# A two-layer kernel gets a written instruction order for TensorE and SyncE in the rest of its first layer, later stores, a weight reload on another queue, and wider spacing in its attention part

## The chip, the cores and the metric

One NeuronCore of one Trainium2 chip runs the whole program. The metric is device microseconds of that core, from launch to end; a lower number is better. Engines run side by side, each taking its own instructions in the order in which the program holds them: TensorE (PE in the profile, its weight loads PEld), VectorE (DVE), ScalarE (ACT), GpSimd (POOL) and SyncE (SP), which here only issues transfers. A DMA queue belongs to the engine that issues it.

## The reference, cut to what matters

```python
kv  = einsum('bhsd,bhse->bhde', k, v)            # 8 batches, 8 heads, 576 tokens, 64 wide
out = einsum('bhsd,bhde->bhse', q, kv)
x   = out / sqrt(mean(out*out, -1) + 1e-6) * g_norm    # then (4608 tokens, 512)
h   = x @ w_in;   x = (h * sigmoid(1.702 * h)) @ w_out       # layer 0: 512 -> 2048 -> 512
h   = x @ w2_in;  y = (h - tanh(h)) @ w2_out                 # layer 1: the same sizes
```

## The kernel before, in words

The 4608 tokens are eight superblocks of 576 (`T`; `H` is half of it), one per batch. The program runs layer 0 over superblocks 0 to 7, then layer 1 over the same eight: `for l in range(2): for n in range(NS)` (L876). Between the layers the activations wait in HBM (`x2d`).

**The two matrix stages.** Each matrix product is done on 2 x 2 blocks with seven block products in place of eight, and each operand is split into a float16 high and low part, so a block product is three matmuls of 128 x 288 (high by high, high by low, low by high). `m1` (L520) is the first matrix of a superblock: 54 steps of six matmuls, each into one of the PSUM tiles X, Y, Z, and two more steps (`tail1`, `tail2`) that are emitted among the first steps of the next stage. Its weights `wi[0..7]` stay in SBUF. After a step ACT copies X out (L563), DVE adds Y or Z to a copy (L568), and ACT applies the layer's function into `GT` (L537, L541). `m2` (L635) is the second matrix: 28 steps of twelve matmuls (L702 to L704). Its right operands `jt` are made from `GT` by DVE (`jA`, L591), ACT (`jB`, L605) and DVE again (`jC`, L611), emitted up to six steps ahead in a ring of seven. Its weights are streamed from HBM: `stream` (L629) loads half of a block into one of four slots `st`, 14 loads a superblock, each waiting until TensorE has read the slot's last content. A load emitted in step i is first used about seven steps later. `fin` closes a block product: ACT scales it into a buffer of `mscr`, DVE adds (L650), `store` sends it to `x2d` on SP's queue in layer 0 and to the output `outT` on GpSimd's in layer 1 (L647).

**Side work.** Generators hold the rest of the work; each `yield` is a turn. `tick(0)` after every step of `m1` and `tick(1)` after every step of `m2` give each generator its rate of turns (`add_side(g, rate in m1, rate in m2)`), and what a turn emits stands behind the latest main instruction of the same engine (`issue_after`). In layer 0, `front(b)` is the attention of batch b: four units, each five matmuls for k by v (L385, recorded as ten), two turns, two matmuls by q (L397, recorded as four), ACT squares and copies (L409 to L411), a turn, a DVE subtraction (L413), two turns, four matmuls that sum squares (L421). `back(b)` (L473) is its normalisation: the inverse root (`newton`, L441), then per unit two matmuls that spread it over the partitions (`scaled_unit`, L456) into `AT`, two DVE multiplications that read `AT` (L460), and after every second unit the seven sums and the split that make the next superblock's operand `xo` (`xprep`, L306). From superblock 2 on, `back(n + 1)` runs in `m1` at rate 0.6 and `front(n + 2)` in `m2` at rate 1.1. In superblock 0 both run for batch 1, at 0.15 turns a tick in its first stage and 2.5 in its second, in superblock 1 for batch 2. `conv1` converts layer 1's weights in the `m1` stages from superblock 2 on, with loads and stores on GpSimd's queue, and leaves them in HBM (`wid`, `wod[1]`). After the last `m2` of layer 0, eight transfers of 896 KB on SP's queue bring `wid` into `wi` (L947 to L949).

**What sets the order.** The program is built with a planner that simulates a timeline and picks each engine's order from it, within dependencies. Where `tc.manual_schedule(engines=...)` is open, the named engines keep the order in which the program emits their instructions. Before, that holds for PE and SP in layer 1 alone (L908 to L912):

```python
            if l == 1:
                fixed[0] = True
                ...
                man.enter_context(tc.manual_schedule(engines=frozenset([mybir.EngineType.PE, mybir.EngineType.SP])))
```

Of the kernel before, what the change touches and what calls it, by code (L numbers as in the profile page):

```python
# [21 lines left out]
NS = NTOK // T  # L22
H = T // 2
NP = 8
# [58 lines left out]
def body(ctx, tc, att, gn, con, w_in, w_out, w2_in, w2_out, outT):  # L83
# [217 lines left out]
    def main(ins):  # L301

        latest[ins.ins.engine] = ins.ins
# [51 lines left out]
    def fetch(b):  # L355

        kb = yield from part(b, 0, T, UNIT)
        qb = yield from part(b, 0, 0, T)
        ahead[b] = qb, kb
# [113 lines left out]
    def back(b, dst):  # L473

        hi, hl = shr[:, 0:H], slr[:, 0:H]
        yield from newton(slice(0, P), hi, hl)
        for x in yt:
            x.free()
        for u, (kt, i) in enumerate(UNITS):
            yield from scaled_unit(b, u, hl, slice(0, P), AT)  # L480
            if i == 1:
                ex = yield from scr.need(3 * H)
                yield from xprep(xbs[b, kt], ex, dst[:, kt])
                if kt == 0 and b < NS - 1:
                    yield from fetch(b + 1)


    side, fixed = [], [False]
# [146 lines left out]
    def m2(l, n, tails, pre):  # L635
        inv = 1.0 / (SX * SW[1])
        cc = {}
        tail1, tail2, flush = tails
        LA = NJ - 2

        def store(qd, ob, ds):

            m, j = qd // 2, qd % 2
            src = ob.ap[:, :T].rearrange("p (d f) -> p d f", d=2)[:, ds]
            dst = (x2d if l == 0 else outT.rearrange("(k p) f -> k p f", p=P))
            dst = dst[2 * m:2 * m + 2, :, n * T + j * H:n * T + (j + 1) * H].rearrange("d p f -> p d f")[:, ds]
            main((nc.sync if l == 0 or n == NS - 1 else nc.gpsimd).dma_start(out=dst, in_=src))  # L647

        def fma(out, ps, b):
            main(nc.vector.scalar_tensor_tensor(out=out, in0=ps, scalar=inv, in1=b, op0=ALU.mult, op1=ALU.add))  # L650

        def scaled(ps, d, name):
            if d == 0:
                cc[name] = mscr(T)
            o = cc[name].ap[:, d * H:(d + 1) * H]
            main(nc.scalar.activation(out=o, in_=ps, func=AF.Copy, scale=inv))
            return o

        def quad(qd, d, name):
            if (l, n) == (1, NS - 1):  # L660
                store(qd, cc[name], slice(d, d + 1))
            elif d == 1:
                store(qd, cc[name], slice(0, 2))
            if d == 1:
                cc.pop(name).free()

        def fin(r, d):
            x, y, z = X[d][:, 0:H], Y[d][:, 0:H], Z[d][:, 0:H]
            if r == 1:
                o = scaled(x, d, 1)  # L670
                fma(o, y, o)
                quad(0, d, 1)
            elif r == 6:
                o = scaled(x, d, 6)
                fma(o, z, o)
            elif r == 7:
                o = scaled(x, d, 7)
                fma(o, z, o)
                quad(3, d, 7)
            elif r == 3:  # L680
                o = cc[6].ap[:, d * H:(d + 1) * H]
                fma(o, y, o)
                quad(1, d, 6)
            elif r == 4:
                scaled(x, d, 4)
                quad(2, d, 4)

        for i in range(28):
            r, pp = STEPS2[i]
            s = pre[ORDER2.index(r) * 2 + pp // 2]  # L690
            jadvance(i + 1)
            j = jbuf.pop(i)
            bank = {2: Y, 1: X, 5: Z, 6: X, 7: X, 3: Y, 4: X}[r]
            fresh = r in (2, 1, 5, 3)
            k = not fresh
            for d in range(2):
                out = bank[d][:, 0:H]
                for p in range(2):
                    wh, wl = (s[:, pp % 2 * 2 + p, d, t, :] for t in range(2))
                    xh, xl = (j[:, p, t, :] for t in range(2))  # L700
                    a, z = fresh and i == FIRST2[r] and p == 0, i == LAST2[r] and p == 1
                    nc.tensor.matmul(out=out, lhsT=wh, rhs=xh, start=a, stop=False, skip_group_check=k)  # L702
                    nc.tensor.matmul(out=out, lhsT=wh, rhs=xl, start=False, stop=False, skip_group_check=k)  # L703
                    nc.tensor.matmul(out=out, lhsT=wl, rhs=xh, start=False, stop=z, skip_group_check=k)  # L704
                if i == LAST2[r]:
                    fin(r, d)
            for _ in range(min(FREED2.get(i, 0), 14 - len(pre))):
                pre.append(stream(l, len(pre)))
            if i == 0:
                tail1()  # L710
            elif i == 1:
                tail2()
            elif i == 2:
                flush()
                flush()
                jcap[0] = 28
            jadvance(i + 1 + LA)
            tick(1)


    QW = {(0, 0): 1, (0, 1): 2, (1, 0): 3, (1, 1): 0}
# [154 lines left out]
    for l in range(2):  # L876
        for n in range(NS):
            bk = fr = None
            if l == 0:
                if n == 0:  # L880
                    bk = add_side(both(1, xo[1]), 0.15, 2.5)
                elif n == 1:
                    bk = add_side(both(2, xo[0]), 1.5, 0.8)
                elif n < NS - 1:
                    bk = add_side(back(n + 1, xo[(n + 1) % 2]), 0.6, 1.0)
                else:
                    bk = add_side(x2load(0, xo[0]), 0.4, 0.8)
            elif n < NS - 1:
                bk = add_side(x2load(n + 1, xo[(n + 1) % 2]), 0.4, 0.8)
            if (l, n) == (0, 2):  # L890
                add_side(later, 0.85, 0.0)

            def hook(p):
                if (l, n) == (0, 0):
                    adv((16, 18, 20, 21, 22, 23, 24, 25)[p])
                    if p == 2:
                        withdraw(extra)
                    return
                if (l, n) == (0, 1):
                    upto(p + 2)  # L900
                if p >= 2 and p % 2 == 0:
                    jcap[0] = (1, 2, 5)[p // 2 - 1]
                    jadvance(jcap[0])

            jpos[:] = [0, 0, 0]
            jcap[0] = 0
            man = ExitStack()
            if l == 1:  # L908
                fixed[0] = True
                marks.clear()  # L910
                marks.update({k: m for k, m in latest.items() if k == mybir.EngineType.DVE})
                man.enter_context(tc.manual_schedule(engines=frozenset([mybir.EngineType.PE, mybir.EngineType.SP])))  # L912
            if (l, n) == (0, 0):
                m1_plain(hook)
                adv(32)
                k4 = lambda t, n: [t[:, k * 1024:k * 1024 + 1024] for k in range(n)]
                dfr = []
                late = k4(jx, 2)

                def start_sums():  # L920
                    for p in range(NP):
                        for h in range(2):
                            nc.sync.dma_start(out=wod[0][0:3, :, p, h].rearrange("r q t f -> q r t f"), in_=wi[p][:, h, 4:7])
                    for p in range(0, NP, 4):
                        nc.sync.dma_start(out=wod[0][3, :, p:p + 4], in_=w3[:, p:p + 4])
                    spare.extend(k4(cbk, 3) + k4(stf, 2) + late)
                    dfr.append(add_side(sums(), 1.5, 0.7))
                m2_plain()
                drain([bk])
                barred.extend(late)  # L930
                spare[:] = [x for x in spare if all(x is not e for e in late)] + k4(stf[:, 2048:4096], 2)
                closed.append(1)
                jn[0] = sn[0] = 0
                continue
            if (l, n) == (0, 1):
                upto(2)
            tails = m1(l, n, hook)
            if (l, n) == (0, 1):
                drain(dfr)
            jcap[0] = 5  # L940
            pre = [stream(l, i) for i in range(4)]
            if l == 0 and 1 <= n < NS - 2:
                drain([bk])
                fr = add_side(front(n + 2), 0.0, 1.1)
            m2(l, n, tails, pre)
            if l == 0 and n == NS - 1:
                drain([later])  # L947
                for p in range(NP):
                    nc.sync.dma_start(out=wi[p], in_=wid[p])  # L949
            drain([bk, fr])  # L950
            man.close()

# [40 lines left out]
```

## Time and profile before

| | |
|---|---|
| median of 3 runs | 1512.32 us (1511.89 to 1515.27) |
| the profiled execution's own time | 1515.95 us |
| its span, first to last instruction | 1514.2 us |
| TensorE busy | 1459.4 us (96%), 11508 matmul records |
| VectorE, ScalarE, GpSimd busy | 1184.3 us (78%), 945.7 us (62%), 134.7 us (9%) |
| mean granted TensorE clock | 0.981 of full speed |

The profile is of one execution. Times in it count from the first instruction. A matmul's recorded length (0.29 us) is longer than the distance to the next one's start, since matmuls overlap; the pace is read from start to start. In rows with an idle time, it stands in brackets with what ended it. Layer 0 ends and layer 1 begins near 851 us; superblock 2 of layer 0 begins near 285 us.

### The profile page before, as it was taken

How to read it: one execution, taken by the hardware profiler on the slowest of the kernel's cores; microseconds unless marked ns; L12 is line 12 of the kernel's file. 1: busy time of each engine (PE TensorE's matmuls, PEld its weight loads, DVE VectorE, ACT ScalarE, POOL GpSimd, SP SyncE). 2: the span in 40 equal slices, each digit the busy share in tenths (PEclk: the TensorE clock that was granted, in tenths of full speed). 3: DMA queues.
4: the chain of work that ended last, by engine and by line, in shares of the span. 5: the costliest groups of instructions: out<-in, count | busy, mean ns of one | idle time of the engine just before them, and what ended most of it. 6: DMA issues, size and time to landing. Idle time of an engine off the chain costs nothing.

```text
span 1514.2 us, 29446 instructions
## 1 busy us (share of the span) xinstructions
PE 1459.4 (96%) x11508; PEld 1159.8 (77%) x11508; DVE 1184.3 (78%) x2357; ACT 945.7 (62%) x2075; POOL 134.7 (9%) x209
## 2 busy tenths in 40 slices
PE   6979799999999999999999999999999999999999
PEld 5667577777787877877677777777777777777777
DVE  4999979497796987959858686877777787868585
ACT  5766586676777767767556465646565565656463
POOL 0000010022223221211100000000000000000000
PEclk8899899999999999999999999999999999999999
DMA  8684415447567475672576415070614333241504
GB/s 310 208 249 128 147 62 196 140 132 250 165 209 234 128 253 178 199 237 70 185 250 231 148 59 192 15 231 22 195 56 156 111 118 125 86 142 44 184 15 157
DMA packets 96525, 235.36 MB, mean 155 GB/s; under 512 B 10112, under 2 KB 49152, under 8 KB 96384
## 3 DMA queue, kind: packets, MB, share of 16 engines
q1 hardware_dynamic: 78848, 165.95, 34.1%
q0 software_dynamic: 17536, 67.51, 13.4%
q8 instruction: 90, 1.47, 0.4%
q14 instruction: 51, 0.42, 0.1%
HBM read 191.48 MB, written 41.94 MB: 154 GB/s over the span
## 4 chain that ended last, share of the span: by engine, by line
PE 78%; DMA 8%; DVE 8%; ACT 3%; issue 3%; POOL 0%; SPq 0%; ACTq 0%; DVEq 0%; POOLq 0%
PE X L530 7%; PE X L702 7%; PE X L704 7%; PE X L703 7%; PE X L532 7%; PE X L531 7%; PE Y L702 4%; PE Y L704 4%; PE Y L703 4%; PE Z L530 3%; PE Z L532 3%; PE Z L531 3%; DMA st<-wod 3%; PE Z L702 2%; PE Z L704 2%
## 5 line engine op out<-in xcount | busy, mean ns | idle before, releaser
L611 DVE SCALAR_TENSOR_TENSOR jt<-gt,jt 128x576 f16<-128x576 f32 x420 | 312.6, 753 | 106.9 <-ACT jt L605 103.1
L605 ACT ACTIVATE jt<-gt 128x576 f16<-128x576 f32 x420 | 284.6, 684 | 156.0 <-PE X L704 56.6
L530 PE MATMUL X<-xo,wi 128*128 128x288 f16 x960 | 274.6, 286 | 7.4 <-ACT mscratch L563 4.7
L531 PE MATMUL X<-xo,wi 128*128 128x288 f16 x960 | 274.7, 286 | 2.1 <-DVE xo L323 2.1
L532 PE MATMUL X<-xo,wi 128*128 128x288 f16 x960 | 274.6, 286 | 0.0
L703 PE MATMUL X<-jt,st 128*128 128x288 f16 x960 | 274.2, 286 | 0.0
L704 PE MATMUL X<-jt,st 128*128 128x288 f16 x960 | 274.0, 286 | 0.0
L702 PE MATMUL X<-jt,st 128*128 128x288 f16 x960 | 273.4, 286 | 0.0
L702 PEld LDWEIGHTS <-st 128*128 128x128 f16 x1680 | 165.0, 98 | 60.8 <-DMA st<-wod 17.2
L563 ACT COPY mscratch<-X 128x288 f32<-128x288 f32 x360 | 141.2, 396 | 106.1 <-PE X L532 92.6
L531 PEld LDWEIGHTS <-wi 128*128 128x128 f16 x1680 | 164.7, 98 | 50.4 <-issue 8.2
L530 PEld LDWEIGHTS <-wi 128*128 128x128 f16 x1680 | 164.5, 98 | 47.1 <-issue 4.4
L703 PEld LDWEIGHTS <-st 128*128 128x128 f16 x1680 | 165.1, 98 | 43.4
L704 PEld LDWEIGHTS <-st 128*128 128x128 f16 x1680 | 165.2, 98 | 43.4 <-issue 0.3
L532 PEld LDWEIGHTS <-wi 128*128 128x128 f16 x1680 | 164.5, 98 | 44.3 <-issue 2.5
L591 DVE TENSOR_TENSOR gt<-gt 128x576 f32<-128x576 f32 x240 | 176.7, 749 | 1.4 <-ACT gt L537 1.1
L702 PE MATMUL Y<-jt,st 128*128 128x288 f16 x480 | 136.2, 289 | 10.3 <-DMA st<-wod 10.3
L568 DVE TENSOR_TENSOR mscratch<-Z,mscratch 128x288 f32<-128x288 f32 x240 | 108.1, 452 | 38.5 <-ACT mscratch L563 22.2
L703 PE MATMUL Y<-jt,st 128*128 128x288 f16 x480 | 137.9, 288 | 0.0
L704 PE MATMUL Y<-jt,st 128*128 128x288 f16 x480 | 137.5, 288 | 0.0
L530 PE MATMUL Z<-xo,wi 128*128 128x288 f16 x480 | 137.5, 286 | 0.0
L531 PE MATMUL Z<-xo,wi 128*128 128x288 f16 x480 | 137.4, 286 | 0.0
(238 smaller groups left out, 2572.0 us busy)
## 6 DMA issues: line engine op xcount, KB each, us to landing
st<-wod SPq DMA_DIRECT2D x210, 512.0 KB, 4.7
scratch<-att POOLq DMA_DIRECT2D x28, 640.0 KB, 4.8
scratch<-x2d SPq DMA_DIRECT2D x32, 288.0 KB, 5.9
cbk<-w_out POOLq DMA_DIRECT2D x32, 256.0 KB, 4.3
cbk<-w_in POOLq DMA_DIRECT2D x32, 256.0 KB, 4.1
scratch<-att POOLq DMA_DIRECT2D x28, 288.0 KB, 4.5
x2d<-mscratch SPq DMA_DIRECT2D x28, 288.0 KB, 5.4
outT<-mscratch POOLq DMA_DIRECT2D x28, 288.0 KB, 5.0
```

The source lines that it names most:

```text
L530: nc.tensor.matmul(out=out, lhsT=wh, rhs=xh, start=fresh and kt == 0, stop=False, skip_group_check=k)
L531: nc.tensor.matmul(out=out, lhsT=wh, rhs=xl, start=False, stop=False, skip_group_check=k)
L532: nc.tensor.matmul(out=out, lhsT=wl, rhs=xh, start=False, stop=kt == 1, skip_group_check=k)
L563: main(nc.scalar.copy(out=b.ap, in_=x))
L568: main(nc.vector.tensor_tensor(out=b.ap, in0=add[0], in1=b.ap, op=ALU.add))
L591: tt = lambda o, a, b: main(nc.vector.tensor_tensor(out=G[:, :, o, :], in0=G[:, :, a, :], in1=G[:, :, b, :], op=ALU.subtract))
L605: main(nc.scalar.activation(out=j[:, :, 0, :], in_=GT[STEPS2[i][1]][:, :, QD[STEPS2[i][0]], :], func=AF.Copy, scale=SX))
L611: main(nc.vector.scalar_tensor_tensor(out=j[:, :, 1, :], in0=GT[STEPS2[i][1]][:, :, QD[STEPS2[i][0]], :], scalar=SX, in1=j[:, :, 0, :], op ...
L702: nc.tensor.matmul(out=out, lhsT=wh, rhs=xh, start=a, stop=False, skip_group_check=k)
L703: nc.tensor.matmul(out=out, lhsT=wh, rhs=xl, start=False, stop=False, skip_group_check=k)
L704: nc.tensor.matmul(out=out, lhsT=wl, rhs=xh, start=False, stop=z, skip_group_check=k)
```

## The change

- From superblock 2 of layer 0 on (`n >= 2`), PE and SP keep the order of emission, as in layer 1.
- In layer 0 a `store` is no longer emitted where its block product is finished: it is put on a list and emitted three steps later, behind that step's weight loads (`due`); the last one at the stage's end. Its buffer is given back then.
- `back` gets two more turns after `newton` and one more after each unit (six in all); its rate in `m1` from superblock 2 to 6 is 0.72 in place of 0.6.
- The reload of `wi` between the layers is a generator on GpSimd's queue, given 0.4 turns a step during the last `m2` of layer 0, in place of eight transfers on SP's queue emitted after it; what is left of `conv1` is emitted before that `m2`, not after it.

```diff
@@ back
         for x in yt:
             x.free()
+        yield
+        yield
         for u, (kt, i) in enumerate(UNITS):
             yield from scaled_unit(b, u, hl, slice(0, P), AT)
+            yield
             if i == 1:
...
+    def reload():
+
+        for p in range(NP):
+            nc.gpsimd.dma_start(out=wi[p], in_=wid[p])
+            yield
@@ m2, store
-            main((nc.sync if l == 0 or n == NS - 1 else nc.gpsimd).dma_start(out=dst, in_=src))
+            if l == 0:
+                late.append((step_[0] + 3, dst, src, ob))
+            else:
+                main((nc.sync if n == NS - 1 else nc.gpsimd).dma_start(out=dst, in_=src))
@@ m2, quad
-                cc.pop(name).free()
+                ob = cc.pop(name)
+                if l == 1:
+                    ob.free()
@@ m2
+        step_, late = [0], []
+
+        def due(i):
+            while late and late[0][0] <= i:
+                _, dst, src, ob = late.pop(0)
+                main(nc.sync.dma_start(out=dst, in_=src))
+                ob.free()
+
         for i in range(28):
+            step_[0] = i
...
             for _ in range(min(FREED2.get(i, 0), 14 - len(pre))):
                 pre.append(stream(l, len(pre)))
+            due(i)
...
             tick(1)
+        due(99)
@@ the loop over superblocks
-                    bk = add_side(back(n + 1, xo[(n + 1) % 2]), 0.6, 1.0)
+                    bk = add_side(back(n + 1, xo[(n + 1) % 2]), 0.72, 1.0)
...
                 man.enter_context(tc.manual_schedule(engines=frozenset([mybir.EngineType.PE, mybir.EngineType.SP])))
+            elif n >= 2:
+                man.enter_context(tc.manual_schedule(engines=frozenset([mybir.EngineType.PE, mybir.EngineType.SP])))
...
-            m2(l, n, tails, pre)
             if l == 0 and n == NS - 1:
                 drain([later])
-                for p in range(NP):
-                    nc.sync.dma_start(out=wi[p], in_=wid[p])
+                fr = add_side(reload(), 0.0, 0.4)
+            m2(l, n, tails, pre)
             drain([bk, fr])
             man.close()
```

## Rows read from the trace of the kernel before

**Rows 1.** The page's head: span, TensorE's busy time, its granted clock in 40 slices.
```profile
span 1514.2 us, 29446 instructions
...
PE 1459.4 (96%) x11508; PEld 1159.8 (77%) x11508; DVE 1184.3 (78%) x2357; ACT 945.7 (62%) x2075; POOL 134.7 (9%) x209
...
PEclk8899899999999999999999999999999999999999
```
**Rows 2.** Stretches: length, each engine's busy us (count), PE's clock, DMA share, GB/s.
```profile
528.00:578.00 50.00, 47.54 (x361) 38.04 (x359) 38.47 (x70) 35.01 (x73) 10.10 (x16) 0.97 0.78 254
1099.00:1472.00 373.00, 373.00 (x3043) 297.49 (x3041) 282.83 (x552) 210.60 (x457) 12.13 (x17) 1.00 0.32 103
```
**Rows 3.** Waits of TensorE from 285 to 851: us in total, times, longest.
```profile
PE Y L702 <- DMA st<-wod: 9.1, 5, 2.5
PE Z L702 <- DMA st<-wod: 4.4, 2, 2.3
PE X L530 <- ACT mscratch L563: 0.4, 2, 0.2
```
**Rows 4.** TensorE's timeline around one of those waits: start, length, instruction.
```profile
736.67 0.32 PE L702 MATMUL Z<-jt,st 128*128 128x288 f16 x1 [2.29 <-DMA st<-wod]
736.80 0.43 PE L703 MATMUL Z<-jt,st 128*128 128x288 f16 x1
...
740.14 0.33 PE L702 MATMUL Z<-jt,st 128*128 128x288 f16 x1
```
**Rows 5.** TensorE's timeline, two more of those waits.
```profile
349.78 0.30 PE L702 MATMUL Z<-jt,st 128*128 128x288 f16 x1 [2.09 <-DMA st<-wod]
...
832.87 0.30 PE L702 MATMUL Y<-jt,st 128*128 128x288 f16 x1 [2.03 <-DMA st<-wod]
833.00 0.29 PE L703 MATMUL Y<-jt,st 128*128 128x288 f16 x1
```
**Rows 6.** The chain of waits, 723 to 742: start, length, what.
```profile
730.61 6.01 DMA st<-wod
```
**Rows 7.** Weight loads (L632), 285 to 851: from issue to landing.
```profile
DMA to landing us min/median/max: 3.7/4.9/8.8
```
**Rows 8.** Waits of SP's queue from 285 to 851: us in total, times, longest.
```profile
SPq L647 <- DVE mscratch L650: 16.1, 13, 3.1
```
**Rows 9.** Timelines of one attention unit: q matmuls on TensorE, subtraction on DVE.
```profile
444.12 1.13 PE L397 MATMUL AT<-scratch,kv 128*128 128x288 f32 x4
448.80 0.75 DVE L413 TENSOR_TENSOR sq<-scratch,sq 128x576 fp32r<-128x576 f32 x1
```
**Rows 10.** The quickest and the slowest such pair, on TensorE and DVE.
```profile
566.51 1.13 PE L397 MATMUL AT<-scratch,kv 128*128 128x288 f32 x4
569.08 0.76 DVE L413 TENSOR_TENSOR sq<-scratch,sq 128x576 fp32r<-128x576 f32 x1 [0.40 <-ACT sq L410]
...
373.40 1.13 PE L397 MATMUL AT<-scratch,kv 128*128 128x288 f32 x4
378.97 0.76 DVE L413 TENSOR_TENSOR sq<-scratch,sq 128x576 fp32r<-128x576 f32 x1 [3.16 <-ACT sq L410]
```
**Rows 11.** Timelines of spread matmuls and the multiplications that read them.
```profile
687.84 0.52 PE L456 MATMUL AT<-sq,sel 128*128 128x288 f32 x2
688.59 0.81 DVE L460 TENSOR_TENSOR scratch<-AT,scratch 128x288 f32<-128x288 f32 x2
...
596.54 0.52 PE L456 MATMUL AT<-sq,sel 128*128 128x288 f32 x2
600.96 0.81 DVE L460 TENSOR_TENSOR scratch<-AT,scratch 128x288 f32<-128x288 f32 x2
```
**Rows 12.** Waits of TensorE from 156 to 236.
```profile
PE X L530 <- ACT mscratch L563: 4.0, 5, 1.8
PE X L531 <- DVE xo L323: 2.1, 1, 2.1
PE X L530 <- ACT xo L320: 2.0, 1, 2.0
```

## The prediction, written before the result was known

> **What bounds the kernel now.** The page first: TensorE is busy 96% of the 1514.2 us span, and its clock is below full in the first fifth alone [rows 1]. Slices hide short losses, so next the table of stretches. In layer 1 TensorE is busy for all of 373.00 us with 3043 matmuls, 0.1226 us each, at full clock [rows 2]. That is the floor for this list of matmuls; layer 1, already in written order, has nothing to give. In layer 0 a stretch of 50 us has 47.54 us of work and a clock of 0.97 [rows 2]: here time is lost.
>
> The waits of TensorE from 285 to 851 us say to what: seven waits for a weight load, 9.1 + 4.4 = 13.5 us, and next to nothing else (0.4 us for ACT) [rows 3]. The chain of waits shows where one comes from: the load was issued at 730.61, the moment its slot was free, and took 6.01 us [rows 6], but TensorE wanted it 2.29 us before 736.67 [rows 4], less than four microseconds after the issue. A step of `m2` is 12 x 0.1226 = 1.47 us, and by emission a load is first used some seven steps after its slot is free, 10.3 us. So the planner's order of matmuls, which starts block products early and interleaves them, uses up the distance that the program had put there.
>
> Each wait has a second price. After 736.67 the matmuls from 736.80 to 740.14 start 0.24 us apart [rows 4], the 1.2 GHz level; then 2.4 GHz comes back. The same follows the waits near 350 (2.09 us), 556 and 654. It does not follow the one of 2.03 us at 832.87 [rows 5]. One such stretch costs half its length, 3.34 / 2 = 1.67 us; four make 6.7 us.
>
> **Part by part.** *PE and SP in order, gain.* The seven waits go if each load has its 10.3 us: landing takes 4.9 us in the median and 8.8 at most [rows 7], so even the slowest has 1.5 us left. I take all of it: 13.5 us of waiting, 6.7 us of clock, 0.4 us for ACT: 20.6 us. What is late next is below.
>
> *Late stores.* On an SP queue in order, a store waiting for DVE would hold the loads behind it. Waits for DVE before a store are at most 3.1 us [rows 8]; three steps are 4.4 us, and the loads of the same step go first. So a store finds its data ready: no cost to the loads. It isn't later for the buffer's next user either, since the last two stores follow the last load and go when their data is there. Zero; were a store still to wait 3.1 us, the load behind would have 8.8 + 3.1 = 11.9 us to fit into 10.3 in the very worst case, 1.6 us each.
>
> *Reload on GpSimd.* Eight issues off SP's queue onto one with 134.7 us of work in 1514.2 [rows 1], given out over 20 of 28 steps; the first has over 30 us before layer 1 reads it, and the slowest landing of a 512 KB load is 8.8 us [rows 7]. Zero, hidden behind the last `m2` of layer 0. Without that cover, layer 1's first step would wait for one landing, up to some 9 us.
>
> *PE in order, price in `front`.* Now the attention's matmuls stand at fixed places. Between q matmuls and square sums lie three turns; at 1.1 turns a step that is three steps in two of the four units and two steps in the other two. With the q matmuls themselves (1.13 us) TensorE comes to the square sums 5.5 or 4.1 us after it began on q. The subtraction they need is done after 569.84 - 566.51 = 3.3 us at best, 379.73 - 373.40 = 6.3 us at worst [rows 10], 5.4 us in an ordinary unit [rows 9]. So a two-step unit waits between nothing and 2.2 us, a three-step unit between nothing and 0.8. There are 16 units from superblock 2 on, eight of each kind. With 0.5 us for the first kind and 0.15 for the second (latencies lie between the ordinary and the best, as ACT and DVE no longer have steps of `m2` begun early to serve): 5 us; bounds 0 and 8 x 2.2 + 8 x 0.8 = 24 us.
>
> The Trainium skill, page "TensorE: Matmul & The Clock Gate", section "Step-by-step: what each phase is for", says that only weight loads are pulled ahead and that matmuls stay in program order. By that rule every matmul behind an unready square sum waits with it, though it could run; this speaks against the change, and is the third rival below. The trace agrees as far as it goes: at 736.67 all of TensorE stood 2.29 us for one operand.
>
> *PE in order, price in `back`.* Each second spread must wait until `AT` is read. At 0.72 turns a step of 6 x 0.1226 = 0.74 us, three turns are about four steps: with the spread's own 0.52 us TensorE is back after 3.5 us. The multiplications end 1.6 us after the spread began where DVE comes straight to them, and 5.2 us after where the sums of `xprep` are still in front [rows 11]. In order, `xprep` is emitted before that spread, so the first is the nearer row. Ten such pairs: 2 us, bounds 0 and 10 x 1.7 = 17.
>
> *PE in order, price in `m1`.* X must be copied out within two steps, 1.5 us. With the planner's order this cost 0.4 us in six superblocks [rows 3], but 4.0 us in superblock 1, where ACT was as loaded [rows 12]. Five superblocks carry the conversion of weights: I take 2 us, bounds 0 and 20.
>
> *Six turns more in `back`.* In superblock 0 it makes the operand for which TensorE already waits at the start of superblock 1: 2.1 + 2.0 us on `xo` [rows 12]. Six turns at 2.5 a tick are 2.4 ticks, and a tick there stands for twelve matmuls, 1.47 us: some 4 us of later emission. But the planner places these instructions, and DVE's backlog sets much of their time: 1.5 us, bounds -2 (a luckier plan of the first 285 us) and 4.
>
> **Sum.** -20.6 + 5 + 2 + 2 + 1.5 = -10.1 us on the profiled execution's 1515.95 us: 1505.9. The median of the runs shown is 3.6 us lower, so 1502.2 us; I say 1502.
>
> **Rivals.** *All gained, nothing paid:* layer 1 speaks for it, 373 us without one wait in the same order [rows 2]; against it, layer 1 has no attention and no conversion. 1512.3 - 20.6 = 1491.7 us.
>
> *The wait changes its name:* the prices come near half their bounds together, (24 + 17 + 20) / 3 = 20 us, in pieces too short for the clock to fall: 1512 us. For it speaks DVE's load, 38.47 of 50 us [rows 2]; against, 0.4 us of waiting for ACT in the planner's order.
>
> *Slower, the square sums:* in the eight two-step units the subtraction takes its worst 6.3 us. Each waits 2.2 us, longer than 2.09, after which the clock fell [rows 5], and pays 1.67 us more: 8 x 3.9 = 31 us. With the other prices: 1512.3 - 20.6 + 31 + 5.5 = 1528 us. It decides from about 15 / 8 = 1.9 us a unit. Against it: 6.3 us stands once, in a unit whose DVE was idle for 3.16 us waiting for ACT [rows 10].
>
> *The loads stay late:* the queue in order is held by something I don't see, and the 20.6 us stay while the prices are paid: 1523 us. Layer 1's same queue speaks against it.
>
> **Chances.** Forecast (1497 to 1507) 0.45; all gained (to 1497) 0.20; the wait changes its name (1507 to 1517) 0.20; slower by the square sums 0.12; loads late 0.03. About 0.2%, 3 us, is what a measurement of this kernel can tell from none, so faster is below 1509.3: 0.45 + 0.20 + 0.08 of the third = 0.73. Within: 0.10. Slower: 0.02 + 0.12 + 0.03 = 0.17. The range 1490 to 1517 leaves out the last two cases; the forecast's own is 1497 to 1507.
>
> **What would show it.** Right: no row of TensorE waiting for a weight load between 285 and 851, full clock there, and short waits (under 2 us) on the subtraction (L413) at L421 and on DVE at L456. Superblocks 6 and 7, which have no `front`, should lose their waits whole. Wrong: a weight load among TensorE's waits; a clock under 1.00 after square sums; a first 285 us longer than now by over 4 us; TensorE waiting for `wi` when layer 1 begins.

## The result, and the profile after

The change makes the kernel slower: median 1520.47 us (1515.56 to 1530.33, 20 runs) against 1512.62 us (1506.76 to 1517.88, 20 runs) before, ratio 1.0051 with a 95% interval of 1.0037 to 1.0064. I had forecast 1502 us, faster.

The change does to the weight loads what it says, and the profile shows it. The page's head first, against [rows 1], then the stretch of [rows 2] that held a lost clock (length, busy us of each engine, granted clock, DMA share, GB/s).

```profile
span 1516.6 us, 29456 instructions
...
PE 1459.8 (96%) x11508; PEld 1158.8 (76%) x11508; DVE 1185.8 (78%) x2357; ACT 948.1 (63%) x2075; POOL 140.2 (9%) x217
```
```profile
528.00:578.00 50.00, 48.35 (x377) 39.01 (x376) 41.05 (x76) 36.53 (x78) 10.80 (x17) 1.00 0.82 259
```

The clock is full there now (0.97 before), and the stretch still isn't full of matmuls: 48.35 of 50 us. TensorE's waits from 285 to 853 us say why (us in total, times, longest), against [rows 3]; line numbers have moved, L539 and L725 are L530 and L702 of before.

```profile
PE X L539 <- ACT mscratch L572: 6.5, 11, 2.3
PE AT L421 <- DVE sq L413: 5.1, 6, 1.6
PE Z L539 <- DVE mscratch L577: 2.0, 5, 0.6
PE X L725 <- ACT mscratch L668: 1.7, 4, 0.7
PE AT L421 <- ACT scratch L411: 0.8, 1, 0.8
PE AT L456 <- DVE scratch L460: 0.5, 1, 0.5
```

The seven waits for a weight load (13.5 us) are gone. In their place stand 28 waits, 16.6 us together, for ACT and DVE: X not yet copied out, the square sums' operand not yet there. Such a row counts from the recorded end of the matmul before, which lies 0.29 - 0.12 = 0.17 us past the pace, so 28 waits cost some 28 x 0.17 = 4.8 us more, about 21 us in all (an estimate). The longest of them opens superblock 2. TensorE's timeline (start, length, instruction, idle time before) and ACT's at that moment:

```profile
287.08 0.29 PE L541 MATMUL Y<-xo,wi 128*128 128x288 f16 x1
289.71 0.28 PE L539 MATMUL X<-xo,wi 128*128 128x288 f16 x1 [2.34 <-ACT mscratch L572]
```
```profile
285.64 1.28 ACT L438 ACT_TABLE_LOAD   x1
286.93 0.44 ACT L438 ACTIVATE scratch<-ms 128x288 f32<-128x288 f32 x1
287.41 0.44 ACT L439 ACTIVATE scratch<-scratch 128x288 f32<-128x288 f32 x1
287.87 1.28 ACT L433 ACT_TABLE_LOAD   x1
289.16 0.20 ACT L433 ACTIVATE dummy<-scratch 128x1 f32<-128x1 f32 x1
289.27 0.38 ACT L572 COPY mscratch<-X 128x288 f32<-128x288 f32 x1
```

ACT is taken from 285.64 to 289.36 by the inverse root that ends the attention front of superblock 1: two table loads and three small operations, 3.7 us. The X copy for which TensorE waits comes right behind. In the profile before, ACT does the same from 285.84 to 289.56, and the planner lets TensorE go on with other products. The two stretches, before and after (33 matmuls against 15):

```profile
285.80:289.60 3.80, 3.80 (x33) 3.03 (x31) 0.00 (x1) 3.71 (x7) 0.00 (x0) 1.00 0.71 208
```
```profile
285.60:289.40 3.80, 1.76 (x15) 1.27 (x13) 0.00 (x0) 3.71 (x7) 0.00 (x0) 1.00 0.67 208
```

(The Trainium skill, page "ScalarE: Activation LUTs", section "What ACT_TABLE_LOAD costs", has about 2.66 us for each switch of tables, half of it a drain. Here the next operation starts 1.29 us after the load began, and no drain shows.)

The next longest wait has another cause. ACT, which keeps the planner's order, stood 3.60 us until 341.61 for a load of the weight conversion, with the squares of an attention unit behind it (its q matmuls had ended at 338.26). Of the 5.9 us for square sums, 2.4 come right after, at 343.46 (0.79 us) and at 345.47:

```profile
341.61 0.67 ACT L152 ACTIVATE cbk<-cbk 128x512 f32<-128x512 f32 x1 [3.60 <-DMA cbk<-w_out]
345.47 0.40 PE L421 MATMUL AT<-sq,sel 128*128 128x288 f32 x1 [1.61 <-DVE sq L413]
```

Where the time went, by superblock: lengths in us between the last matmuls of two second stages, read from TensorE's timelines. The columns on the right are experiments told below.

| layer 0, superblock | before | after | order from 6 | order from 3 | ACT relieved | ACT relieved, from 3, turn |
|---|---|---|---|---|---|---|
| 0 and 1 | 285.2 | 285.0 | 284.1 | 284.5 | 285.6 | 286.9 |
| 2 | 99.6 | 103.4 | 97.7 | 96.9 | 102.4 | 96.7 |
| 3 | 95.0 | 98.1 | 96.5 | 99.4 | 97.0 | 96.2 |
| 4 | 98.3 | 98.7 | 95.1 | 100.4 | 96.1 | 95.6 |
| 5 | 98.7 | 98.8 | 99.8 | 99.6 | 95.5 | 96.6 |
| 6 | 89.2 | 85.1 | 86.1 | 85.2 | 83.9 | 85.8 |
| 7 | 84.5 | 82.4 | 82.4 | 82.4 | 82.7 | 82.7 |

In some runs six matmuls (0.7 us) lie on the other side of a border. Superblocks 6 and 7, which have no front, win 6.2 us; 2 and 3 lose 6.8; 4 and 5 come out even; layer 1 takes 1.6 us more. That is the 2.4 us between the two spans. The medians lie 7.9 us apart: the profiled execution of before took 1515.95 us, 3.3 above its median, that of after 1518.61, 1.9 below. So the traces understate the loss by some 5 us, and shares of it are better taken from ratios of many runs, below.

### The profile page after: what moved, and what is told of

Its sections match the earlier page's. It is cut to its first block, busy times and chain, and to the rows that moved or that the text cites. A ratio compares the mean times of both kernels' runs of the same rounds, so it can differ in the third digit from the quotient of the medians.

```text
span 1516.6 us, 29456 instructions
## 1 busy us (share of the span) xinstructions
PE 1459.8 (96%) x11508; PEld 1158.8 (76%) x11508; DVE 1185.8 (78%) x2357; ACT 948.1 (63%) x2075; POOL 140.2 (9%) x217
## 4 chain that ended last, share of the span: by engine, by line
PE 54%; issue 17%; DVE 15%; DMA 7%; ACT 6%; POOL 1%; SPq 0%; ACTq 0%; POOLq 0%; DVEq 0%
PE X L725 5%; PE X L726 5%; PE X L727 5%; PE X L539 4%; PE X L541 4%; PE X L540 4%; DVE gt L600 3%; PE Y L725 3%; PE Y L727 3%; PE Y L726 3%; DVE jt L620 2%; PE Z L539 2%; PE Z L540 2%; PE Z L541 2%; DVE mscratch L577 1%
## 5 line engine op out<-in xcount | busy, mean ns | idle before, releaser
L539 PE MATMUL X<-xo,wi 128*128 128x288 f16 x960 | 274.7, 287 | 13.6 <-ACT mscratch L572 11.2
L725 PE MATMUL X<-jt,st 128*128 128x288 f16 x960 | 274.5, 286 | 2.8 <-ACT mscratch L668 1.7
L541 PE MATMUL X<-xo,wi 128*128 128x288 f16 x960 | 275.1, 287 | 0.0
L727 PE MATMUL X<-jt,st 128*128 128x288 f16 x960 | 274.5, 286 | 0.0
L539 PEld LDWEIGHTS <-wi 128*128 128x128 f16 x1680 | 164.6, 98 | 47.2 <-issue 4.4
L725 PEld LDWEIGHTS <-st 128*128 128x128 f16 x1680 | 164.3, 98 | 44.9 <-DMA st<-wod 2.5
L541 PEld LDWEIGHTS <-wi 128*128 128x128 f16 x1680 | 164.6, 98 | 44.4 <-issue 2.5
L727 PEld LDWEIGHTS <-st 128*128 128x128 f16 x1680 | 164.4, 98 | 41.7
L539 PE MATMUL Z<-xo,wi 128*128 128x288 f16 x480 | 137.7, 287 | 2.1 <-DVE mscratch L577 2.0
L540 PE MATMUL Z<-xo,wi 128*128 128x288 f16 x480 | 137.6, 287 | 0.0
L725 PE MATMUL Y<-jt,st 128*128 128x288 f16 x480 | 136.8, 286 | 0.8 <-DMA st<-wod 0.8
L541 PE MATMUL Z<-xo,wi 128*128 128x288 f16 x480 | 137.5, 286 | 0.0
L726 PE MATMUL Y<-jt,st 128*128 128x288 f16 x480 | 137.2, 286 | 0.0
```

Source lines behind the costliest of these rows:

```text
L539: nc.tensor.matmul(out=out, lhsT=wh, rhs=xh, start=fresh and kt == 0, stop=False, skip_group_check=k)
```

## The experiments

Three theories stood at first. Theory A: the order wins back the weight loads and pays as much or more where TensorE meets the attention and an ACT that is late. Theory B: the order is good and one of the other edits costs. Theory C: SP's order is what counts. Each run is compared with runs of the kernel before on the same chip (medians 1513.1 to 1514.5 us), by ratio with its 95% interval.

### Which edit, which engine, which superblocks

**e1_order_only.** The kernel before, with one edit:
```diff
+            elif n >= 2:
+                man.enter_context(tc.manual_schedule(engines=frozenset([mybir.EngineType.PE, mybir.EngineType.SP])))
```


> The kernel before with only the written order of PE and SP from superblock 2 on; stores, reload and spacing as before. Theory A (the written order wins back about 20 us of weight-load waits and clock, and pays as much or more in superblocks 2 to 5, where TensorE now waits at fixed places for ACT and DVE): the pay is at least that of the full change, since the spreads stand closer and stores stand ahead of loads: 1518 to 1527 us. Theory B (the order is good, one of the other three edits costs): 1500 to 1508 us.

Measured: 1544.2 us, ratio 1.0199 (1.0169 to 1.0228). Far slower than either theory had it. One wait at the start of layer 1 makes ten of the 30 us:
```profile
PE Z L530 <- DMA wi<-wid: 10.0, 1, 10.0
```
The eight reloads stand on SP's queue behind the last `m2`, and now nothing moves them up. Between 283 and 853 us TensorE also waits where the added turns are missing, 5.0 us for the first spread:
```profile
PE AT L456 <- DVE sq L449: 5.0, 5, 1.7
```
So the other edits are what makes the order bearable; theory B has it the wrong way round.

**e2_no_order.** The full change without those two lines. 

> The full change without the written order in layer 0: late stores, reload on GpSimd, spacing and rate stay. Theory A: nothing of size left, 1510 to 1515 us, with waits for weight loads still in the trace. Theory B: the cost is here, 1518 to 1523 us.

Measured: 1515.71 us, ratio 1.0006 (0.9986 to 1.0027): no difference, as theory A had it (its band ended 0.7 us lower). Weight loads are waited for again, 9.4 us in this execution, its three lines' sum:
```profile
PE Y L725 <- DMA st<-wod: 6.2, 5, 3.6
PE Z L725 <- DMA st<-wod: 2.7, 1, 2.7
PE X L725 <- DMA st<-wod: 0.5, 1, 0.5
```

**e3_order_from_6.** `elif n >= 6:`. 

> The full change with the written order only from superblock 6 on, where no attention front runs beside m2. Theory A: superblocks 6 and 7 keep the 6 us that they gain in the trace of the full change, and superblocks 2 to 5 go back to the planner: 1504 to 1509 us, faster than both kernels. Theory B: 1518 us or more, as the other edits stay.

Measured: 1510.47 us, ratio 0.9970 (0.9952 to 0.9988), faster than before, a little over the expected band.

**e4_sp_only.** The full change with the order for SP alone:
```diff
-                man.enter_context(tc.manual_schedule(engines=frozenset([mybir.EngineType.PE, mybir.EngineType.SP])))
+                man.enter_context(tc.manual_schedule(engines=frozenset([mybir.EngineType.SP])))
```


> The full change with the written order for SP alone in layer 0; TensorE goes by the planner. Theory A: weight loads are late because TensorE takes them early, so the waits for them stay, 8 us or more between 285 and 851, and the time is 1508 to 1516 us. Theory C (the loads were late because SP's queue was badly ordered): their waits fall under 3 us without the new waits on ACT and DVE, 1495 to 1503 us.

Measured: 1513.50 us, ratio 0.9996 (0.9978 to 1.0014), and the loads are waited for as before:
```profile
PE Y L725 <- DMA st<-wod: 6.7, 5, 2.5
PE Z L725 <- DMA st<-wod: 5.0, 3, 2.7
```
Theory C falls. The loads were late because TensorE took them early.

### What the price is made of

**e5_front_turn.** One turn more before the square sums, and the rate that makes room for it:
```diff
+            if b > 3:
+                yield
             for j in range(2):
                 w = sel[:, 98 - 32 * u - 2 * j:226 - 32 * u - 2 * j]
...
-                fr = add_side(front(n + 2), 0.0, 1.1)
+                fr = add_side(front(n + 2), 0.0, 1.3 if n > 1 else 1.1)
```


> The full change with one more turn between the DVE subtraction and the square sums of the attention front, for the batches whose front runs under the written order, at 1.3 turns a step in place of 1.1: at least three steps of m2 lie between q matmuls and square sums in every unit. Theory A (TensorE waits at places that are written too close to what ACT and DVE can deliver): the waits at L421, 5.9 us in the full change's trace, fall under 2 us, nothing else grows, and the time falls by 3 to 5 us, to 1515 to 1518. Theory D (superblocks 2 to 5 are bound by ACT and DVE with TensorE in a fixed order, so a wait taken away comes back at X copies or elsewhere): the waits at L421 fall, but the sum of the waits from 285 to 851 stays within 2 us of 16.6, and so does the time.

Measured: 1520.16 us, ratio 1.0039 (1.0021 to 1.0057): not told apart from the full change. Its waits of TensorE from 283 to 853 (L541 and L727 are the X matmuls of the two stages):
```profile
PE X L541 <- ACT mscratch L574: 7.1, 10, 2.3
PE X L727 <- ACT mscratch L670: 2.6, 5, 0.7
PE AT L397 <- ACT kv L389: 2.4, 1, 2.4
PE AT L423 <- DVE sq L413: 2.0, 2, 1.6
PE Z L541 <- DVE mscratch L579: 1.4, 4, 0.6
PE AT L423 <- ACT scratch L411: 0.2, 1, 0.2
```
The square sums wait 2.2 us in place of 5.9, as planned, and ACT's lines take most of it back: 15.7 us in all, against 16.6. Sum and time are as theory D had them, but its reason, that ACT and DVE bind superblocks 2 to 5, isn't what the trace shows: superblocks 3 to 5 get shorter by 4.0 us together (97.4, 97.4 and 96.8), and superblock 2 alone longer by 3.8 (107.2). There the 2.4 us at L397 stand behind ACT's wait for a load of the conversion, and the clock falls behind the table loads' wait (last section).
```profile
374.41 0.66 ACT L152 ACTIVATE cbk<-cbk 128x512 f32<-128x512 f32 x1 [5.53 <-DMA cbk<-w_out]
```

**e6_order_m1** and **e7_order_m2.** In superblocks 2 to 5 the order holds in one stage alone: it is closed after `m1`, or opened there (with `elif n >= 6:` above).
```diff
             tails = m1(l, n, hook)
+            if l == 0 and 2 <= n < 6:
+                man.close()
```


> The full change with the written order in superblocks 2 to 5 in the first stage alone. Theory A: the price of the first stage (X and Z copies, about 8 us) is paid, and the waits for weight loads of the second stage come back (about 5 us in four superblocks): 1516 to 1522 us. Theory D: the same direction, no difference.

> The full change with the written order in superblocks 2 to 5 in the second stage alone, 6 and 7 whole. Theory A: no weight load is waited for, the price in the first stage goes, that of the square sums stays (6 to 8 us): 1509 to 1514 us. Theory D: the waits at L421 and at X in m2 grow by what the first stage no longer pays, and the time stays at 1518 us or above.

Measured: e6 1512.62 us, ratio 0.9989 (0.9973 to 1.0005); e7 1522.25 us, ratio 1.0047 (1.0028 to 1.0065). e6 came out below its band; e7's time is in theory D's band, though its square sums (5.2 us, ACT's part included) wait no more than in the full change. Against the order from superblock 6 on (e3), the first stage costs some 3 us, the second some 12 (each uncertain by about 4). So the rows of the full change, 8.5 us of them in the first stage, tell where TensorE waits, and not which stage's order makes ACT late. In e7 the largest wait is not at the square sums but at the first step of superblock 6, which stands ahead of the end of the second stage before it: 3.5 us near 673.
```profile
PE Z L539 <- DVE mscratch L662: 4.4, 2, 3.5
PE X L725 <- ACT mscratch L668: 3.6, 5, 1.7
PE AT L421 <- DVE sq L413: 3.1, 4, 0.9
```
The timelines of ACT and TensorE there:
```profile
669.15 0.66 ACT L152 ACTIVATE cbk<-cbk 128x512 f32<-128x512 f32 x1 [6.31 <-DMA cbk<-w_in]
672.69 0.28 PE L539 MATMUL Z<-xo,wi 128*128 128x288 f16 x1 [3.46 <-DVE mscratch L662]
676.63 1.28 ACT L438 ACT_TABLE_LOAD   x1
```
ACT had stood 6.31 us for a load of the conversion, DVE 6.59 us behind ACT, and TensorE behind DVE. The front's table loads come only after. From 674 to 682 us the granted clock is 0.57.

**e8_m2_turn.** e7 with the two edits of e5. 

> The last two edits together: written order in the second stage of superblocks 2 to 5, whole in 6 and 7, and the extra turn before the square sums. Theory A: neither weight loads nor square sums are waited for in size, 1503 to 1508 us, faster than both kernels and than the order from superblock 6 on. Theory D: 1510 us or above.

Measured: 1511.64 us, ratio 0.9971 (0.9952 to 0.9990). Here the same edits win 10 us, though the time stays in theory D's band. The long wait near 673 is gone; the square sums still wait 5.4 us, so it isn't their turn that won. Nor do the table loads come earlier: in superblock 5 they begin 8.0 us before the stage's last matmul, in e7 10.6. ACT stands for the conversion's loads about as long in both (22.2 us here, 22.9 in e7), but at other places, and at most 4.1 us at once. Why the edits win here and not in e5 stays open; that the planner's places for these operations merely fell better is not ruled out.

**e9_front3_early.** The same cure for the start of superblock 2: `1.6 if n == 1 else 1.1`. 

> The full change with the attention front of superblock 1 (batch 3, not under the written order) at 1.6 turns a step in place of 1.1. Theory E: the largest part of the price is one place, the start of superblock 2, where ACT is still at the two activation-table loads that end this front (3.7 us) while TensorE, in order, needs X copied: 2.3 us of waiting, a clock that falls in some executions, and a late start of what follows. With the front done earlier superblock 2 falls from 102 to 107 us to about 97, and the time to 1513 to 1516 us. Theory F (the price is spread over superblocks 2 to 5 alike): no change, 1518 to 1522 us.

Measured: 1521.57 us, ratio 1.0053 (1.0033 to 1.0074). The edit did not do what it should: the wait of 2.34 us stands where it stood, now at 288.28. That front is in the planner's hands, which does not follow the rate. So e9 tells nothing of the place.

**e10_order_from_3.** `elif n >= 3:` takes the place out. 

> The full change with the written order from superblock 3 on. Theory E: superblock 2 under the planner takes about 97 us and the time is 1513 to 1516 us. Theory F: a quarter of the price goes, 1517 to 1519 us; or the same wait moves to the start of superblock 3.

Measured: 1514.64 us, ratio 1.0013 (0.9995 to 1.0031). Superblock 2 takes 96.9 us, and nothing of its size comes at the start of superblock 3. Theory F falls, and theory E is right in the place. In the cause it is right in part: TensorE's rows in superblock 2 of the full change add up to 6.8 us, of which 2.3 stand behind the table loads and 2.4 behind ACT's wait at 341.61. e10 takes all of them away together.

**e11_both.** e9 and e5 together. 

> The full change with the early front of superblock 1 and, for superblocks 2 to 5, the extra turn before the square sums at 1.3 turns a step. Theory E: both prices go, 1509 to 1514 us. Theory F: 1518 us or above, as with the extra turn alone.

Measured: 1518.66 us, ratio 1.0039 (1.0017 to 1.0062); as e5, since e9's edit did nothing.

### ACT's load

**e12_conv_pool.** Two of ACT's operations per piece of weight conversion go to GpSimd (32 pieces, mean 1.88 and 1.13 us there):
```diff
-        nc.scalar.activation(out=av, in_=rf[:, :, 1], func=AF.Copy, scale=2.0 ** -111)
+        if l:
+            nc.gpsimd.tensor_scalar(out=av, in0=rf[:, :, 1], scalar1=2.0 ** -111, scalar2=None, op0=ALU.mult)
+        else:
+            nc.scalar.activation(out=av, in_=rf[:, :, 1], func=AF.Copy, scale=2.0 ** -111)
...
-            nc.scalar.copy(out=d[:, :, 0, :], in_=B[:, 1:8])
+            nc.gpsimd.tensor_copy(out=d[:, :, 0, :], in_=B[:, 1:8])
```


> The full change with the two ACT operations of each piece of layer 1's weight conversion (scale copy of 512, cast of 896 columns, 0.67 and 0.94 us) on GpSimd. Theory A, the part on m1: ACT's load is what makes X copies late; their waits in superblocks 3 to 6 fall by half or more, and the time by 2 to 4 us. Rival G: the copies wait behind bursts of jt and xo operands on ACT, not behind the conversion: the waits and the time stay within 1 us. Or GpSimd's operations stand in front of the attention's loads on its queue, and TensorE waits for those: slower.

Measured: 1509.98 us, ratio 0.9977 (0.9964 to 0.9990): 10 us better than the change alone, more than expected, and faster than before. TensorE's waits from 283 to 853, all above 0.2 us:
```profile
PE AT L424 <- DVE sq L416: 4.6, 5, 1.7
PE X L542 <- ACT mscratch L575: 3.8, 5, 2.3
PE Z L542 <- DVE mscratch L580: 0.6, 2, 0.4
```
X waits 3.8 us, 2.3 of them at the start of superblock 2, so 1.5 elsewhere against 4.2 in the full change; the waits for X in the second stage are gone. The edit takes two things from ACT: 38 us of work (busy 352.0 us from 285 to 853, 390.4 in the full change), and the place where it stood for the conversion's loads (6.5 us in the full change, none here; GpSimd stands for them now, 5.6 us, and no row of TensorE names it). No run parts the two, so "ACT relieved" means both.

**e13_before_pool.** The same edit on the kernel before. 

> The kernel before with the two ACT operations of the weight conversion on GpSimd, nothing else. Theory H (the written order is what needs ACT free; the planner goes around a late ACT): within 3 us of before, 1511 to 1517 us. Rival I (ACT's load costs under any order): as much is won as on the full change, 1503 to 1508 us.

Measured: 1528.53 us, ratio 1.0102 (1.0072 to 1.0132). Rival I falls, and theory H was too mild: under the planner the edit costs 15 us.
```profile
PE Y L705 <- DMA st<-wod: 8.2, 5, 2.0
PE Z L705 <- DMA st<-wod: 4.7, 2, 3.2
PE AT L388 <- DMA scratch<-att: 4.5, 2, 3.1
PE X L533 <- ACT mscratch L566: 3.7, 5, 2.1
```
The weight loads, 14.2 us with a third row of 1.3, are hardly waited for more than before (13.5). New are waits for the attention's operands, whose loads share GpSimd's queue with the new work, and for X and Z copies (3.7 and 1.6 us, 0.4 for ACT before). Why the planner's order suffers more was not tried.

**e14_pool_from_3**: e12 with `elif n >= 3:`. **e15_pool_from_3_turn**: that with the two edits of e5.

> The full change with the conversion's ACT operations on GpSimd and the written order from superblock 3 on. Theory E (the start of superblock 2 is one place that costs some 5 us): 1503 to 1507 us. If ACT's relief already covers that place: 1508 to 1511 us.

> The last one with the extra turn before the square sums at 1.3 turns a step. With ACT relieved the waits at the square sums (3 to 5 us) should go without coming back elsewhere: 1500 to 1505 us. If they come back at X copies, as they did with ACT loaded: the same as the last one.

Measured: e14 1507.43 us, ratio 0.9956 (0.9938 to 0.9974); e15 1505.26 us, ratio 0.9940 (0.9920 to 0.9959). e14 lies between its two bands. e15 has the lowest median of all and is faster than both kernels; from e14, 2 us above it, it is not told apart. e15's waits of TensorE from 283 to 853:
```profile
PE X L544 <- ACT mscratch L577: 3.4, 7, 0.9
PE Z L544 <- DVE mscratch L582: 0.8, 2, 0.6
PE AT L388 <- DMA scratch<-att: 0.5, 1, 0.5
PE AT L426 <- DVE sq L416: 0.5, 2, 0.3
PE Y L730 <- DMA st<-wod: 0.4, 1, 0.4
PE Y L544 <- DVE mscratch L582: 0.2, 1, 0.2
```
5.8 us in all, 8.1 in e14. With ACT relieved, the extra turn takes the square sums' wait away in the trace (3.2 us in e14, 0.5 here) and nothing comes back.

**e16_pool_from_1.** e12 with the order opened in the second stage of superblock 1 too. 

> The full change with the conversion's ACT operations on GpSimd and the written order from the second stage of superblock 1 on. Theory E: the front of superblock 1 then ends some five steps before superblock 2 begins, the 2.3 us wait behind the table loads is gone, superblock 2 takes 96 to 98 us, and the time is 1502 to 1507 us. Rival: the front's operands (its loads, DVE) aren't ready at the written places of superblock 1, and it pays more there than it saves: 1510 us or above.

Measured: 1518.48 us, ratio 1.0039 (1.0023 to 1.0055): the rival. Superblock 2 does fall to 97.5 us, but superblock 1 pays ten, half of it in one wait for the attention's loads (160 to 285 us):
```profile
PE AT L388 <- DMA scratch<-att: 8.7, 3, 5.1
```

## Why the prediction was wrong

By ratios, the written order counts like this: none 1.0006, from superblock 6 0.9970, from 3 1.0013, from 2 1.0051. So it wins some 5 us in superblocks 6 and 7, loses some 6 in 3 to 5, and some 6 in superblock 2 alone (differences of ratios on 1513 us, each uncertain by 3 to 4). In the traces the gain came and the prices ate it: some 21 us of waits (16.6 by the rows) against 9 us forecast for `front`, `back` and `m1`. The signs that I had named for "right" came true (no weight load waited for, full clock, short waits at L421 and L456, superblocks 6 and 7 shorter) and none of those for "wrong" did. None of them watched the X copies.

- *Gain of the order, 20.6 us.* The mechanism was right: no weight load is waited for from 285 to 853 and the clock is full. The size was that of one execution: e2 and e4, with TensorE in the planner's order, wait 9.4 and 11.7 us where the profile of before waits 13.5. So some 2 to 4 us of it may be too many.
- *Late stores and reload, zero.* Right together, within 3 us (e2, 1.0006); and e1 shows what the reload's cover was worth, 10 us.
- *`front`, 5 us.* Right in size, 5.9 us, wrong in part in the cause. I set it by turns against latencies; 2.4 us of it stand behind ACT's wait for a load of the conversion. The worst pair of [rows 10], 6.3 us, which I took for a latency, was such a place too: ACT came to its squares 2.09 us late in the profile of before.
```profile
376.67 0.67 ACT L152 ACTIVATE cbk<-cbk 128x512 f32<-128x512 f32 x1 [2.09 <-DMA cbk<-w_out]
```
- *`back`, 2 us; six turns, 1.5 us.* 0.5 us at L456, and superblocks 0 and 1 end at 285.0 in place of 285.2: nothing.
- *`m1`, 2 us out of bounds 0 and 20: the step that failed.* I took the waits under the planner (0.4 us) for the nearer row and superblock 1's 4.0 us [rows 12] for the far one. X and Z copies wait 8.5 us, four times the forecast, and the second stage's X, which I had not counted, 1.7. The largest single wait of these, 2.3 us, is the table loads at the start of superblock 2, which I had not looked for. That superblock costs 6 us in all by e10, 3 by e14 against e12, where ACT is relieved; the table loads are one part of it. With ACT relieved, the X and Z copies wait 4.4 us in e12. How much of the rest is ACT's work and how much its standing for loads is open.
- *The rivals.* "The wait changes its name" was the right one, at 1512 us. Its prices, 20 us, are close to the 21 paid, and from 285 to 853 us the clock stayed full, as it said. That the median lies 8 us above it, beyond its band's end at 1517, is for the larger part what stays open below. The slower rival, square sums at 2.2 us each, did not come: seven waits of 0.3 to 1.6 us.

What stays open besides: the last 5 us between the traces' 2.4 and the medians' 7.9. No trace here shows an execution at after's median and one at before's side by side.

## What to carry to other kernels

An order written by hand is only as good as the slowest engine that feeds it is early. Before fixing TensorE's order, count what the feeding engines carry at each step, and look for the places where one of them, in its own order, stands for a transfer (3.6 us at once here, 6.3 in e7): what is behind it comes late. Moving such work off ACT brought the change from 1.0051 to 0.9977, and with a later start and one turn more to 0.9940. Under the planner's order the same move lost 15 us, so it is no gain by itself. Waits that a planner avoids leave no row; the list of short waits of the planner's trace is no measure of what a fixed order will pay. And look at where an engine is taken for long at a stretch (3.7 us of table loads): in a fixed order, that place should lie where its consumers are some steps ahead (argued, not shown: e16 moved it so, won there and paid more elsewhere).

## What the runs showed of the hardware that I had not expected

The clock does not follow the length of a wait alone. After 2.34 us near 288 us the profile of after keeps its full clock; the same wait in e5, which ends 0.74 us later, is followed by a stretch at 1.2 GHz (granted clock 0.79 over the window). The stretch from 288 to 296 us in both, after first:
```profile
288.00:296.00 8.00, 6.29 (x52) 5.04 (x52) 5.04 (x12) 5.29 (x13) 0.00 (x0) 1.00 0.15 55
```
```profile
288.00:296.00 8.00, 5.66 (x33) 3.82 (x32) 2.71 (x7) 5.28 (x13) 0.00 (x0) 0.79 0.24 76
```
The window holds 52 matmuls of the one and 33 of the other; six of the 19 are the later end of the wait. So the 2.03 us and 2.09 us of [rows 5], which I read as two sides of a bound, are none.
